# Linear attention and SwiGLU in one kernel: two stretches of small-tile matmuls of group 1 joined into one

## The chip, the cores and the metric

One core of one Trainium2 chip. The metric is device microseconds from the first to the last instruction of the core as the host sees it, median of several executions; a traced execution also has a span, which is 1.7 to 1.9 us shorter. The engines are called PE (TensorE; PEld is its loading of weights), DVE (VectorE), ACT (ScalarE), POOL (GpSimd) and SP (the sync engine, which here issues DMA). PSUM is the memory that PE writes its results to, in banks; SBUF is the memory that holds operands.

## The reference, cut to what matters

```python
def phi(x):
    return np.where(x > 0, x, np.exp(x) - 1.0) + 1.0
q_p, k_p = phi(q), phi(k)                            # 8 batches, 8 heads, 576 x 64
kv  = np.einsum('bhsd,bhse->bhde', k_p, v)           # "k.v": one 64x64 result per head
z   = np.sum(k_p, axis=2)
num = np.einsum('bhsd,bhde->bhse', q_p, kv)          # "q.kv"
den = np.einsum('bhsd,bhd->bhs', q_p, z) + 1e-06     # "q.z"
x   = num / den                                      # 4608 tokens x 512
out = (silu(x @ w_gate) * (x @ w_val)) @ w_out       # "first layer", "second layer"
```

The tokens are worked on in 9 groups of 512. The two layers are matmuls of the full 128x128 array with 512 moving columns, called large here. The attention products k.v, q.z and q.kv use 64x64 tiles of the array, called small. Attention for later tokens is slipped in between the four tiles of a group's second layer.

## The kernel before

A k.v of one batch is 72 small matmuls; both k.v and the products with q are issued by these helpers:

```python
def kv_corner(b, lp, t, first, last):
    ps = kvp[b]
    for j in range(J):                       # J = 9
        for l2 in range(2):
            for hh in range(2):              # four 64x64 corners of the array
                rows = slice(C * hh, C * hh + C)
                nc.tensor.matmul(out=ps[hh][D * l2:D * l2 + D, D * lp:D * lp + D],
                                 lhsT=t[b % 2][rows, lp, j, D * l2:D * l2 + D],
                                 rhs=vr[b % NB][rows, 2 * lp + l2, D * j:D * j + D],
                                 start=(first and j == 0), stop=(last and j == J - 1))

def kv_all(b):                               # k.v of batch b
    kvp[b] = pair()                          # next pair of PSUM banks of a ring of four
    for lp in range(2):
        kv_corner(b, lp, kp, True, True)

def num(g, lp):                              # q.kv
    ps = nump[(g, lp)] = pair()
    ...
```

`r_copy` copies k.v from PSUM to SBUF as R, here with ACT; q.kv uses R as its weights. The block of group 1 (`b1` = 2, `b2` = 3):

```python
def block(g):
    b1, b2 = g + 1, g + 2
    if b1 == 2:
        kv_all(b2)
        for lp in range(2):
            corners(kvp[b2], Zr[1], 1, lp, 7, 9, 2 * P + P * lp)      # q.z
        lnrd(kvp[b2], 0, 2 * P, 4 * P)                                # 1/den on ACT
        for lp in range(2):
            num(b1, lp)                                               # q.kv
            ...
        r_copy(b2, 0, 2, "AA")
...
    for t in range(4):                       # tiles of the second layer
        ...
        if t == 1 and g == 1:
            kv_all(b1)
            r_copy(b1, 0, 2, "AA")
        if t == 3:
            block(g)
        ...
        lay2(g, t)                           # 12 large matmuls
        l2_out(g, t, ...)
```

## Time and profile before

| | kernel before |
|---|---|
| median time | 313.73 us (313.45 to 314.19, 3 runs) |
| span of the traced execution | 311.8 us |
| PE busy, granted clock | 305.4 us (98%), 0.997 |
| DVE, ACT busy | 205.1 us, 152.7 us |
| second layer of group 1, first matmul of tile 0 to first of tile 3 | 70.08 to 80.07 us: 9.99 us |
| the same to the first large matmul of group 2 | 70.08 to 82.78 us: 12.70 us ("the stretch") |

PE is busy throughout and ends the chain, so the question is not which engine is the slowest but what stands in PE's queue and with which gaps. The lines for this are in the prediction.

### The profile page before, as it was taken

The page shows a single profiled execution, that of the slowest core. Times are in us where ns is not written, and L with a number is a line of the kernel's source. Part 1 is how long each engine was busy: PE and PEld are TensorE (multiplying, and loading weights), DVE is VectorE, ACT ScalarE, POOL GpSimd, SP SyncE. Part 2 cuts the span into 40 slices and gives each one's busy share as a digit, 9 for nine tenths or more (in the row PEclk, how much of TensorE's full clock was granted, in tenths as well). Part 3 has the DMA queues.
Part 4 walks back from the last instruction along what each step waited for, and adds up shares of the span by engine and source line. Part 5 has one row for each costly group of instructions (what it writes and reads, how often), then busy time and mean ns, then how long its engine had stood idle before and what let it go on. Part 6 is the DMA issues. An engine that isn't in the chain of part 4 may idle for free.

```text
span 311.8 us, 5565 instructions
## 1 busy us (share of the span) xinstructions
PE 305.4 (98%) x2206; PEld 142.0 (46%) x2206; DVE 205.1 (66%) x361; ACT 152.7 (49%) x231; POOL 48.7 (16%) x73
## 2 busy tenths in 40 slices
PE   7999999999999999999999999999999999999994
PEld 3444454444544454445444544454444444444442
DVE  4855878999599658976697759874981434143410
ACT  4865959538733844374536643574330333033311
POOL 8745444400000410041000500000000000000000
PEclk9999999999999999999999999999999999999998
DMA  8999999999502593239512990323032300240014
GB/s 216 196 198 200 206 206 236 235 206 148 116 15 39 98 196 109 40 58 189 156 38 41 132 233 13 63 52 87 0 75 60 78 1 1 45 92 0 2 34 101
DMA packets 41178, 32.80 MB, mean 105 GB/s; under 512 B 16448, under 2 KB 36160, under 8 KB 41152
## 3 DMA queue, kind: packets, MB, share of 16 engines
q0 software_dynamic: 20480, 18.29, 37.4%
q1 hardware_dynamic: 20592, 14.13, 19.1%
q8 instruction: 17, 0.28, 0.3%
q14 instruction: 9, 0.07, 0.1%
q10 hardware_dynamic: 80, 0.03, 0.0%
HBM read 37.75 MB, written 9.44 MB: 151 GB/s over the span
## 4 chain that ended last, share of the span: by engine, by line
PE 95%; DVE 2%; DMA 1%; SPq 0%; issue 0%; ACT 0%; DVEq 0%
PE pp L292 58%; PE pp L299 30%; PE pp L276 2%; PE pp L254 2%; PE pp L185 2%; DMA q<-in_q_dram 1%; DVE qT L454 1%; PE pp L124 1%; DVE xT L425 0%; PE pp L412 0%; PE pp L212 0%; PE pp L374 0%; DVE osb L322 0%; SPq L333 0%; DVE qp L467 0%
## 5 line engine op out<-in xcount | busy, mean ns | idle before, releaser
L120 ACT ACTIVATE sil<-pp 128x512 f16<-128x512 f32 x108 | 63.4, 597 | 100.8 <-PE pp L292 98.4
L292 PE MATMUL pp<-xT,wg 128*128 128x512 f16 x416 | 106.8, 379 | 0.0
L292 PE MATMUL pp<-xT,wv 128*128 128x512 f16 x416 | 106.8, 379 | 0.0
L285 DVE SCALAR_TENSOR_TENSOR hT<-pp,sil 128x512 f16<-128x512 f32 x108 | 72.3, 681 | 48.0 <-PE pp L292 35.3
L299 PE MATMUL pp<-wo,hT 128*128 128x512 f16 (+2 forms) x444 | 97.1, 373 | 0.6 <-DVE osb L322 0.6
L299 PEld LDWEIGHTS <-hT 128*128 128x128 f16 x444 | 41.9, 98 | 49.9 <-issue 2.1
L292 PEld LDWEIGHTS <-wv 128*128 128x128 f16 x416 | 40.7, 98 | 49.1
L292 PEld LDWEIGHTS <-wg 128*128 128x128 f16 x416 | 40.7, 98 | 48.5
L322 DVE TENSOR_SCALAR osb<-pp 128x512 f32<-128x512 f32 (+1 forms) x19 | 12.9, 681 | 31.1 <-PE pp L299 26.7
L120 ACT ACTIVATE osb<-pp 128x512 f32<-128x512 f32 (+1 forms) x18 | 10.3, 574 | 34.8 <-PE pp L299 34.8
L120 ACT ACT_TABLE_LOAD x13 | 16.7, 1283 | 2.5 <-PE pp L292 2.4
L120 ACT ACTIVATE ek<-kr 128x1152 f16<-128x1152 f16 x16 | 17.8, 1157 | 0.1
L710 POOL COPY gate<-qT 128x1 f16<-128x1 f16 x4 | 1.5, 374 | 95.9 <-DMA qT<-qp 95.9
L229 DVE TENSOR_TENSOR qp<-qp,rden 128x1152 f16<-128x1152 f16 x12 | 16.2, 1347 | 0.0
L220 DVE TENSOR_REDUCE den<-prod 128x18 f32<-128x1152 f16 x12 | 16.1, 1342 | 0.0
L120 ACT ACTIVATE eq<-qr 128x1152 f16<-128x1152 f16 x14 | 15.6, 1151 | 0.1
L271 DVE TENSOR_SCALAR xT<-pp 128x512 f16<-128x512 f32 (+1 forms) x14 | 8.8, 667 | 6.8 <-PE pp L254 6.8
L103 POOL DMA_DIRECT2D vr<-in_v_dram x16 | 11.8, 740 | 8.8 <-DMA wo<-in_moe_w_out_dram 2.4
L103 POOL DMA_DIRECT2D kr<-in_k_dram x16 | 11.5, 722 | 7.9 <-DMA wo<-in_moe_w_out_dram 1.9
L159 DVE TENSOR_TENSOR kp<-ek,kp 128x1152 f16<-128x1152 f16 x15 | 11.4, 758 | 0.5
L147 DVE TENSOR_SCALAR ek<-ek 128x1152 f16<-128x1152 f16 x16 | 8.0, 500 | 5.0 <-ACT ek L120 5.0
L103 POOL DMA_DIRECT2D qr<-in_q_dram x14 | 10.1, 724 | 5.6 <-DMA qr<-in_q_dram 2.6
(86 smaller groups left out, 180.0 us busy)
## 6 DMA issues: line engine op xcount, KB each, us to landing
out_dram<-osb SPq DMA_DIRECT2D x70, 128.0 KB, 2.8
kr<-in_k_dram POOLq DMA_DIRECT2D x16, 288.0 KB, 8.7
vr<-in_v_dram POOLq DMA_DIRECT2D x16, 288.0 KB, 9.7
qr<-in_q_dram POOLq DMA_DIRECT2D x14, 288.0 KB, 11.6
wg<-in_moe_w_gate_dram POOLq DMA_DIRECT2D x5, 256.0 KB, 9.5
wv<-in_moe_w_val_dram POOLq DMA_DIRECT2D x5, 256.0 KB, 10.1
q<-in_q_dram SPq DMA_DIRECT2D x2, 576.0 KB, 4.2
wo<-in_moe_w_out_dram POOLq DMA_DIRECT2D x2, 512.0 KB, 12.4
```

The source lines that it names most:

```text
L103: nc.gpsimd.dma_start(out=dst[b % NB][:, 2 * lp:2 * lp + 2, :], in_=src[b].rearrange("(l a) (c j) d -> (a c) l (j d)", a=2, j=J)[:, 2 * lp ...
L120: nc.scalar.activation(out=out, in_=in_, func=func, bias=bias, scale=scale)
L147: nc.vector.tensor_scalar(out=a, in0=a, scalar1=1.0, scalar2=None, op0=ALU.min)
L159: nc.vector.tensor_tensor(out=a, in0=ek[b % 2][:, lp, :, :], in1=a, op=ALU.add)
L185: nc.tensor.matmul(out=ps[hh][D * l2:D * l2 + D, D * lp:D * lp + D], lhsT=t[b % 2][rows, lp, j, D * l2:D * l2 + D], rhs=vr[b % NB][rows, 2 ...
L220: nc.vector.tensor_reduce(out=den[:, c, :], in_=prod[:, :, :].rearrange("p j (l d) -> p (j l) d", d=D), axis=AX.X, op=ALU.add)
L229: nc.vector.tensor_tensor(out=qv, in0=qv, in1=rden[:, c, :].unsqueeze(2).to_broadcast([P, 2 * J, D]), op=ALU.mult)
L271: nc.vector.tensor_scalar(out=dst, in0=ps[l2][:, c0:], scalar1=1.0 / SC, scalar2=None, op0=ALU.mult)
L285: nc.vector.scalar_tensor_tensor(out=hT[g % 2][:, fb, :], in0=ps[1][:, :], scalar=SC, in1=s[:, :], op0=ALU.mult, op1=ALU.mult)
L292: nc.tensor.matmul(out=ps[h][:, :], lhsT=w[:, c, P * fb:P * fb + P], rhs=xT[g % 2][:, c, :], start=(c == 0), stop=(c == 3))
L299: nc.tensor.matmul(out=l2p[(g, t)][:, n0:n1], lhsT=hT[g % 2][:, fb, P * t:P * t + P], rhs=wo[:, fb, n0:n1], start=(fb == 0), stop=(fb == F ...
L322: nc.vector.tensor_scalar(out=o[:, n0:n1], in0=ps[:, n0:n1], scalar1=1.0 / SC, scalar2=None, op0=ALU.mult)
```

## The change

The intent: batch 2's k.v stood alone between tiles 0 and 1, and PE loses time at each change between large and small tiles. Moved into the block, it shares one entry and one exit with the k.v of batch 3, q.z and q.kv. One of the two q.kv now takes over the banks of batch 2's k.v, so the ring of banks comes out as before but for two pairs that change places.

```diff
-    def num(g, lp):
-        ps = nump[(g, lp)] = pair()
+    def num(g, lp, p=None):
+        ps = nump[(g, lp)] = pair(p)
...
         if b1 == 2:
+            kv_all(b1)
+            r_copy(b1, 0, 2, "AA")
             kv_all(b2)
...
-                num(b1, lp)
+                num(b1, lp, kvp[b1] if lp else None)
...
-                if t == 1 and g == 1:
-                    kv_all(b1)
-                    r_copy(b1, 0, 2, "AA")
```

## The prediction

> **What bounds the kernel now.** I read the busy table and the slices of the page first, then the chain of waits in order of time, then the timeline of group 1's second layer, then the matrix engine's waits. From the page:
>
> ```profile
> PE 305.4 (98%) x2206; PEld 142.0 (46%) x2206; DVE 205.1 (66%) x361; ACT 152.7 (49%) x231; POOL 48.7 (16%) x73
> PE   7999999999999999999999999999999999999994
> PEclk9999999999999999999999999999999999999998
> PE 95%; DVE 2%; DMA 1%; SPq 0%; issue 0%; ACT 0%; DVEq 0%
> ```
>
> TensorE (PE) is busy in every slice after the first, at the full granted clock (0.997), and 95% of the chain that ends last is PE work; no other engine is above 66%. Busy alone would not prove that it is never held up, so I asked who PE waited for from 55 to 310 us. The only answer is 0.6 us for an output copy at the very end. So after the start the kernel is one queue of matmuls, and time can only come from what stands in that queue or from gaps between its entries. A large matmul (128x512) starts every 0.216 us: the chain has 96 of them in 20.72 us.
>
> The part that the change touches, in the chain of waits (start, length, what):
>
> ```profile
> 70.24 2.59 PE pp L299 x12
> 72.83 0.73 PE pp L185 x72
> 73.56 5.29 PE pp L299 x24
> 78.85 0.73 PE pp L185 x72
> 79.58 0.55 PE pp L254 x23
> 80.14 2.69 PE pp L299 x12
> ```
>
> L299 is the second layer, four row tiles of 12 large matmuls. Between tiles 0 and 1 stand the 72 small (64x64) matmuls of batch 2's k.v; between tiles 2 and 3 stand the block: 72 of batch 3's k.v and the 24 of q.z and q.kv. So this group has **two islands of small-tile work**, four changes between full-array and 64x64 work. The later groups already have one island each: at 111.43 the chain shows 16 q.kv then 72 k.v in 0.56 + 0.67 = 1.23 us.
>
> What an island costs beyond its own work must be read by starts, because ends of matmuls are modelled. The PE timeline of this stretch (start, length, what):
>
> ```profile
> 70.08 2.75 PE L299 MATMUL pp<-wo,hT 128*128 128x512 f16 x12
> 72.76 0.80 PE L185 MATMUL pp<-vr,kp 64*64 64x64 f16 x72
> 73.50 5.35 PE L299 MATMUL pp<-wo,hT 128*128 128x512 f16 x24
> 78.78 0.80 PE L185 MATMUL pp<-vr,kp 64*64 64x64 f16 x72
> 79.40 0.30 PE L254 MATMUL pp<-qT,Zr 64*64 64x128 f16 x8
> 79.51 0.62 PE L254 MATMUL pp<-qT,R 64*64 64x384 f16 x16
> 80.07 2.76 PE L299 MATMUL pp<-wo,hT 128*128 128x512 f16 x12
> ```
>
> The reader is to see: 12 large ones from 70.08 would let the next start at 70.08 + 12 x 0.216 = 72.67, but the first small one starts at 72.76, 0.09 us late. The isolated island runs to 73.50, so it takes 73.50 - 72.67 = **0.83 us** of the queue. The same 72 matmuls inside the block, followed by more small ones, go from 78.78 to 79.40: **0.62 us**. The entry into the block shows the same lateness: 73.50 + 24 x 0.216 = 78.68 against 78.78, 0.10 us. In the view of waits, the weight loads sit idle 0.42 us before each island, once put down to "issue" and once to the vector engine's sum for z; the same length both times says that it is the change of tile shape, not a missing operand.
>
> **What the Trainium skill says.** "TensorEngine Tiling (Array Packing)", section Key Properties, says that changing the tiling mode, though not the tile, drains TensorE. The trace agrees in kind: 0.09 to 0.10 us is lost on entry, and (0.83 - 0.62) - 0.09 = 0.12 us on exit; the page gives no length. "TensorE: Matmul & The Clock Gate", Part 2 (what happens when you issue a matmul), says that weight loads are pulled ahead of running matmuls while matmuls stay in program order. The trace agrees: a large weight load starts about 0.21 us before its matmul (72.24 against 72.45), but the first small one starts with its own matmul at 72.76. So the stretch cannot be hidden by running ahead. The spec table at the head of the same page calls ScalarE a strict first-in, first-out queue of depth 8, which matters for where the moved copies of R stand on it.
>
> **The change part by part.**
>
> *Work removed or added: none.* The order of instructions has 4414 PE rows in both programs and the same counts elsewhere. On PE, 72 small matmuls move from behind tile 0 to just ahead of batch 3's k.v. On ScalarE (ACT), the two copies of R for batch 2 move from ahead of tile 1's output copy to behind tile 2's and ahead of the logarithms. The vector, GpSimd and sync orders do not differ.
>
> *Buffers.* There are four pairs of PSUM banks. Call them A, B, C, D in ring order at tile 0. Before: tiles 0 and 1 in A, k.v of batch 2 in B, tiles 2 and 3 in C, k.v of batch 3 in D, q.kv in A and B. After: tiles 2 and 3 take B, k.v of batch 2 takes C, q.kv takes A and, by the new argument, C again. The ring that group 2 inherits is the old one with B and C exchanged, so no later matmul gets a more recently used pair than before.
>
> *PE gain.* The isolated island of 0.83 us becomes 0.62 us inside the block: **-0.21 us**, one entry and one exit less.
>
> *New dependency.* The q.kv of batch 2 needs R of batch 2, which was copied at 76.03, more than 3 us ahead of use at 79.51. Now k.v, copy and use follow each other. My timetable for the new kernel, by starts: 36 large ones from 70.08 end at 77.85; plus 0.10 entry, k.v of batch 2 runs 77.95 to 78.57, batch 3's 78.57 to 79.19, q.z 79.19 to 79.30 (79.40 to 79.51 before). R must be there by 79.30. ACT takes tile 2's output from about 0.21 us after 77.85, so 78.06 to 78.66 (0.60 each). It then needs the end of k.v of batch 2. A 256-column matmul that began at 59.61 released ACT at 59.92, 0.31 us later, and 192 fewer columns at 0.216/512 us each take 0.08 us off, so 0.23 us after the last small one's start at 78.56: about 78.79. The two copies took 0.43 us together, so they end at 79.22. A hand-over to PE took about 0.05 us at the start of the kernel (vector result at 14.80, matmul at 14.85). R is usable at about 79.27, 0.03 us ahead of need, too close to call. I put **+0.05 us** on it, between nothing and some 0.15.
>
> *ACT behind it.* The logarithms started 0.32 us after q.z (79.72 against 79.40), so at 79.51 now; the copies end at 79.22 and do not delay them. ACT's chain to x of group 2 shifts left with the block, and its margin stays.
>
> *Sum:* -0.21 + 0.05 = -0.16 us. The tail from 80.07 on is PE alone, so it should come through whole: 313.73 - 0.16 = **313.57 us**.
>
> **The rivals.**
>
> 1. *The R copy becomes a new wait that eats the gain.* For: the margin above is 0.03 us, and ACT is strictly in order behind a 0.60 us output copy. Against: 0.73 us of PE work (batch 3's k.v and q.z) lies between, and the copy is short. If it goes badly, 0.2 to 0.3 us of wait, and the time is 313.7 to 313.9.
>
> 2. *Another operand is late because the block comes 0.2 us earlier.* Batch 3's k is ready on the vector engine at 77.70, and would be needed at 78.57. The transposes of q for batch 2 are issued at 69.2 and 74.8 and land 3.2 to 6.2 us later; as PE used the second by 79.9 it cannot be the 6.2, so it landed at about 78.0 against 79.3. Group 2's x: the vector engine's last multiply starts at 82.74 for two, ending 83.22, and PE wants its third and fourth chunk at 83.21 and 83.43, a margin of 0.2 us for each. That is thin, but it is tied to the logarithms, which move with the block. If the ACT chain moves less than PE, up to 0.2 us is lost: 313.8.
>
> 3. *The drains do not depend on islands as I think*, and 0.83 against 0.62 is the pitch of that particular k.v. Then nothing is gained: 313.73.
>
> 4. *A much larger effect*, of the clock or of DMA. The clock is full throughout and no transfer feeds PE after the start, so a 2% change (6.3 us) has nothing to come from: the whole stretch moved is 0.83 us, 0.26% of the time.
>
> **Range and chances.** The mechanism gives 313.4 to 313.9. Three runs of the kernel before already spread from 313.45 to 314.19, so run to run scatter is larger than the effect; I widen to 313.0 to 314.2 for that. Even the full island would be 0.3%, so within 2% is near certain.
>
> **What would show it.** In the changed kernel's timeline: no small matmuls between tiles 0 and 1, so 36 large ones start without a gap from 70.08 to 77.85; then 144 k.v ones in about 1.24 us, with one idle stretch of weight loads (0.42 us) ahead of them and none between the two batches; tile 3 at about 79.9 instead of 80.07; the first matmul of group 2 at 82.6 instead of 82.78. Rival 1 shows as a wait of q.kv for ACT's copy of R, or as a gap between q.z and q.kv beyond 0.11 us; rival 2 as a gap inside group 2's first eight matmuls. The prediction is wrong if tile 3 starts no earlier than before, or if the later groups' pitch of 0.216 us changes.

## The result, and the profile after

The changed kernel took 313.69 us (median of 4 runs, 313.49 to 314.06), the kernel before 313.59 (4 runs, 313.40 to 314.19). The ratio is 1.0001, with a 95% interval from 0.9984 to 1.0019: the same. (A ratio here is the mean time of one kernel's fast runs over that of the other's of the same rounds, so it is not quite the ratio of the medians.) So the time agrees with the forecast, 313.57, but the forecast was of a small gain, and the trace must say whether it was there.

From the changed kernel's page, the busy row, the slices and the chain:

```profile
PE 305.7 (98%) x2206; PEld 142.5 (46%) x2206; DVE 204.6 (66%) x361; ACT 152.7 (49%) x231; POOL 48.6 (16%) x73
PE   7899999999999999999999999999999999999994
PE 95%; DVE 2%; DMA 2%; SPq 0%; issue 0%; ACT 0%; DVEq 0%
```

Nothing has changed in kind. The span of this execution is 312.3 us against 311.8, and 0.36 us of that is the start: its tile 0 began at 70.44 instead of 70.08. The chain of waits, same columns as in the prediction, over the part that was changed:

```profile
70.61 7.77 PE pp L299 x36
78.38 1.55 PE pp L185 x144
79.93 0.73 PE pp L254 x20
80.66 2.70 PE pp L299 x12
```

The order is as intended: 36 large matmuls with nothing between them, then 144 of k.v, then q.z and q.kv. By starts, from PE's timeline:

```profile
70.44 7.93 PE L299 MATMUL pp<-wo,hT 128*128 128x512 f16 x36
78.31 1.62 PE L185 MATMUL pp<-vr,kp 64*64 64x64 f16 x144
79.74 0.41 PE L254 MATMUL pp<-qT,Zr 64*64 64x128 f16 x8
80.00 0.66 PE L254 MATMUL pp<-qT,R 64*64 64x384 f16 x16
80.59 2.76 PE L299 MATMUL pp<-wo,hT 128*128 128x512 f16 x12
```

Tile 3 starts 80.59 - 70.44 = 10.15 us after tile 0, where it was 9.99 before: **0.16 us later, not 0.16 us earlier**. The stretch to group 2 is 12.86 us, before 12.70. Each part by starts, beside the prediction's timetable (the 36 large ones, 36 x 0.216 = 7.78 us, are equal in all):

| part, us | before | predicted | changed |
|---|---|---|---|
| first entry (before: of the lone k.v) | 0.09 | 0.10 | 0.09 |
| k.v of batch 2 (before: with its own exit) | 0.73 | 0.62 | 0.68 |
| second entry | 0.10 | none | none |
| k.v of batch 3 | 0.62 | 0.62 | 0.76 |
| q.z | 0.12 | 0.11 + 0.05 for R | 0.26 |
| q.kv with the exit | 0.55 | 0.56 | 0.59 |
| sum | 2.21 | 2.06 | 2.37 |

(The sums are taken before rounding.) The second entry and an exit are indeed gone. But the same small matmuls, which need 0.62 us in an island of their own batch, now need more, and q.z twice its time. What holds them up? The view of waits names no engine for it. The copies of R, which I had feared, were done in time. ACT's timeline, with the idle time before in brackets:

```profile
78.42 0.60 ACT L120 ACTIVATE osb<-pp 128x512 f32<-128x512 f32 x1 [1.43 <-PE pp L299]
79.17 0.45 ACT L120 ACTIVATE R<-pp 128x128 f16<-128x128 f32 x2 [0.16 <-PE pp L185]
```

They end at 79.62, before even q.z begins at 79.74, so q.kv cannot have waited for them at 80.00.

Looking at every single start shows where it goes. Small matmuls come in fours, one for each corner of the array: the four start 3 to 4 ns apart, the next four 32 ns after the first of them. After some 50 matmuls the pattern becomes an even 8 to 9 ns, with weight loads at the same pace. And there are holes. This list, worked out from the traced starts, has every gap of 60 ns or more inside the stretch, by the number of the matmul that it precedes:

```
before, lone k.v (72):    none
before, block (96):       84: 137   92: 138
changed (168):            72: 87   102: 79   150: 86   152: 82   156: 117   164: 94
```

The last two of each block are within q.kv, whose 384 columns keep the array busy (137 ns before); they are not losses. The other four are: 87 ns at the junction of the two k.v, and three of about 80 ns, at places where nothing awaited was late. Each less the 8 ns (at the junction 25) that would stand there anyway, they make 0.29 us; the rest of the loss is in shorter gaps. At the junction stands a separate semaphore instruction (a wait that did not fit on the matmul itself, for batch 3's v). The view of k.v's source line, first of the kernel before and then of the changed one, each limited to the block, gives count, duration, and first and last start:

```profile
L185 PEldq EVENT_SEMAPHORE  x1: 51/51/51, 74.8 to 74.8; - x1
```
```profile
L185 PEldq EVENT_SEMAPHORE  x1: 51/51/51, 78.9 to 78.9; - x1
```

Before, PE's sequencer dealt with it at 74.8, four microseconds ahead of use and under large matmuls. Now it comes up at 78.9, exactly at the junction. That gave the theory to test: **in a long stretch of small matmuls PE uses up instructions as fast as its front end (the fetching and handing out of instructions) supplies them, so the reserve that it builds up under large matmuls runs out, and then every delay of the front end shows.** The rivals: a wait for R after all; the new place or banks of k.v; an array that itself slows in long small-tile work; and chance.

### The profile page after: what moved, and what is told of

It reads as the page before. It is cut to its first block, busy times and chain, and to the rows that moved or that the text cites. A ratio compares the mean times of both kernels' runs of the same rounds, so it can differ in the third digit from the quotient of the medians.

```text
span 312.3 us, 5565 instructions
## 1 busy us (share of the span) xinstructions
PE 305.7 (98%) x2206; PEld 142.5 (46%) x2206; DVE 204.6 (66%) x361; ACT 152.7 (49%) x231; POOL 48.6 (16%) x73
## 4 chain that ended last, share of the span: by engine, by line
PE 95%; DVE 2%; DMA 2%; SPq 0%; issue 0%; ACT 0%; DVEq 0%
PE pp L292 58%; PE pp L299 30%; PE pp L276 2%; PE pp L254 2%; PE pp L185 2%; DMA q<-in_q_dram 2%; DVE qT L454 1%; PE pp L124 1%; DVE xT L425 0%; PE pp L412 0%; PE pp L212 0%; PE pp L374 0%; DVE osb L322 0%; DVE qp L467 0%; DVE kp L143 0%; SPq L333 0%
```

## The experiments

"Stretch" is the measure of the table: 12.70 us before, 12.86 changed. The run-to-run scatter of the whole time is larger than what is sought. Most of the experiments are one traced execution each. How far the stretch scatters can be read from the three kernels of experiments 6 and 9 that leave group 1 as it was before: 12.67 us in each.

**1. The changed kernel again.** No edit.

> The changed kernel once more, to see what repeats. Measure, called the stretch here: from the start of group 1's first second-layer matmul to the start of group 2's first first-layer matmul; 12.70 us in the kernel before, 12.86 in the changed one. Theory (the small-tile stretch of 168 matmuls runs ahead of what PE's sequencer can hand it): the same holes at the same places, 0.09 us between the two k.v, 0.12 us in the middle of the second, 0.17 us around the end of q.z; stretch 12.80 to 12.92; time same within 0.1%. Rival (the holes are chance of that one execution): the holes move or vanish, stretch near the 12.49 that the islands alone would give.

Time 313.60 us (5 runs), ratio 1.0006, interval 0.9993 to 1.0018; stretch 12.88 us. The sum repeats, but the places only in part: holes at 63 (82 ns), 72 (86), 111 (84), 112 (85), and none in q.z. So the junction is fixed, the number of other holes is steady at three, and where they fall moves. Chance placement, then, but not a chance loss. One loss more lies just behind the stretch, where the measure does not see it: the third large matmul of group 2 began 0.50 us after the first instead of 0.43. It uses the third chunk of x, and DVE had begun to multiply that chunk only 0.33 us earlier. The same 0.33 us stands there in experiments 5, 7 and 9 (changed kernel), where this matmul was 0.06 to 0.10 us late; where it was on time, the distance was 0.42 us or more. So this was a wait for x, rival 2 of the prediction, in the changed kernel's second traced execution, though not in its first.

**2. q.kv with an old R**, so that it can't wait for the new copy (the result is wrong: relative error 0.41; `p_old` is set once the block of group 1 is reached).

```diff
-                corners(ps, R[b % 3], b, lp, j0, j1, c0)
+                corners(ps, R[1 if b == 2 and g == 2 and p_old[0] else b % 3], b, lp, j0, j1, c0)
```

> The changed kernel, but q.kv of batch 2 reads the R of batch 1, written long before, so it need not wait for the fresh copy (wrong result on purpose). Theory (feed of PE): R was ready at 79.62 and q.z only began at 79.74, so nothing changes; from the first q.z to the first q.kv stays near 0.26 us, stretch near 12.86. Rival (my prediction's rival 1, wait for the copy of R): q.z to q.kv falls to the 0.12 us of the kernel before, and the stretch to about 12.7.

Stretch 12.84 us; holes at 72 (86), 102 (80), 153 (77), 154 (85), 157 (76), 166 (60). From q.z to q.kv is 0.12 us this time, but the holes went one step on, into q.kv. By that single number the rival looked right; by the stretch and the holes it is out: taking the dependency away gained 0.02 to 0.03 us against the changed kernel.

**3. Four large matmuls between the two k.v**, late place and late R kept.

```diff
-            kv_all(b1)
-            r_copy(b1, 0, 2, "AA")
             kv_all(b2)
...
+                if g == 1 and t == 2:
+                    l2_open(g, t)
+                    for fb in range(FB):
+                        if fb == 8:
+                            kv_all(b1)
+                        l2_mm(g, t, fb)
+                    l2_out(g, t, "A")
+                    r_copy(b1, 0, 2, "AA")
+                    continue
```

> The changed kernel with the last 4 large matmuls of tile 2 moved between k.v of batch 2 and k.v of batch 3: two islands again, all else (banks, late R, order on ScalarE) as in the changed kernel. Theory (a long unbroken small-tile stretch outruns the feed): the second island is like that of the kernel before, k.v of batch 3 0.62 us to q.z, q.z 0.12 us to q.kv, stretch about 12.70. Rival (the late place of k.v or its banks slow the block): the holes stay in the second island and the stretch gets longer than the changed kernel's by one island, to about 13.05.

A miss of my own: stretch 13.07 us. I had put the copies of R behind tile 2's output copy on ACT, and there they ran at 79.34 to 79.78; q.kv then really waited (holes of 190 and 170 ns before its first matmuls). It shows what rival 1 of the prediction costs when it does happen, about 0.4 us. Its k.v of batch 3 had no hole. The mended edit moves the line `r_copy(b1, 0, 2, "AA")` up, to follow `kv_all(b1)` inside the loop:

> The run with 4 large matmuls between the two k.v again, mended: there the copies of R stood behind tile 2's output copy on ScalarE, ran at 79.34 to 79.78 and made q.kv wait; here they stand ahead of it. Theory (PE's front end runs dry in a small-tile stretch longer than about 100 matmuls, and 4 large ones let it fill again): no hole over 60 ns but the two of the kernel before, k.v of batch 3 0.62 us, q.z 0.12 us, stretch 12.70. Rival (late place or banks of k.v): stretch near 12.9 or above.

Stretch 12.70 us, that of the kernel before to the nanosecond (12.696). PE's timeline:

```profile
69.97 7.07 PE L299 MATMUL pp<-wo,hT 128*128 128x512 f16 x32
76.97 0.80 PE L185 MATMUL pp<-vr,kp 64*64 64x64 f16 x72
77.70 1.04 PE L299 MATMUL pp<-wo,hT 128*128 128x512 f16 x4
78.67 0.80 PE L185 MATMUL pp<-vr,kp 64*64 64x64 f16 x72
79.29 0.30 PE L254 MATMUL pp<-qT,Zr 64*64 64x128 f16 x8
79.40 0.62 PE L254 MATMUL pp<-qT,R 64*64 64x384 f16 x16
79.96 2.76 PE L299 MATMUL pp<-wo,hT 128*128 128x512 f16 x12
```

The k.v of batch 2 comes after 32 of the 36 large matmuls, in the same banks. R was copied 1.0 us ahead of q.kv, where the changed kernel left 0.4 us; that the age of R does not matter is what experiment 2 showed. With four large matmuls between, k.v of batch 3 takes 0.62 us again (78.67 to 79.29) and q.z 0.11. So neither place, banks nor R is the cause; the length of the unbroken stretch is, by this execution and by experiment 7.

**4. One island cut into twelve.** In the kernel before, batch 2's k.v is spread over tiles 0 and 1, 4 or 8 small matmuls after every second large one.

```diff
+                    for fb in range(FB):
+                        l2_mm(g, t, fb)
+                        if fb % 2 == 1:
+                            i = 6 * t + fb // 2
+                            for u in range(3 * i // 2, 3 * (i + 1) // 2):
+                                kv_unit(b1, u)
```

> The kernel before with batch 2's 72 k.v matmuls cut into 12 islands, one after every second large matmul of tiles 0 and 1, instead of one. Theory (each entry and exit costs 0.21 us as read): 11 x 0.21 = 2.3 us longer, stretch about 15.0, time 315.9, ratio about 1.007. Rival (the 0.21 us is not the change of shape but something of that one island): stretch near 12.7 and the same time.

Time 316.03 us against 313.50, ratio 1.0082 (1.0066 to 1.0097); stretch 15.16 us. Eleven more islands cost 15.16 - 12.70 = 2.46 us, 0.22 us each; the time agrees, 2.53 us. The price of entry and exit in the prediction (0.21) was right, and is seen by the clock, not only in the trace.

**5. The waits of the junction taken ahead**, by a dummy matmul inside tile 2 that waits for batch 3's v, half of its k and the bank:

```diff
+                        if fb == 8:
+                            nc.tensor.matmul(out=ring[1][0][:, 448:512], lhsT=kp[1][:, 0, 8, :],
+                                             rhs=vr[0][:, 1:3, 0:32], start=True, stop=True)
```

> The changed kernel plus one dummy matmul inside tile 2 that waits for batch 3's v, for its first half of k and for the bank, so that the weight loads at the junction of the two k.v carry no wait (its result is not read). Theory (waits of the junction are handled by PE's sequencer in line, 51 ns for the separate semaphore instruction): the junction falls from 87 ns to about 22 ns, the dummy costs about 0.05 us, the holes of about 80 ns further on stay; stretch about 12.85. Rival (the junction is a real wait for data): it stays at 87 ns or more.

The junction fell from 87 to 25 ns, the dummy cost 29 ns, and two holes of 85 and 89 ns stayed (at 110 and 111); stretch 12.81 us. So the 87 ns were the handling of a wait for something long there, not the wait.

**6. The effect made large enough for the clock.** In groups 2 to 5 of the kernel before, 72 more k.v matmuls (`kv_dup`: the previous batch's, into other columns, not read) either join the block of 88 or stand as an island between tiles 1 and 2.

```diff
                 # in the block
+                kv_dup(b1, ring[0])
                 kv_all(b2)
...
                 # or, in the other kernel, ahead of tile 2
+                if t == 2 and g > 1 and b2 < B:
+                    kv_dup(b1, ring[2])
```

> The effect made large enough for the clock: the kernel before with 72 more k.v matmuls (the previous batch's, result not read) in the blocks of groups 2 to 5, in one stretch with the 88 that stand there. Theory (front end runs dry): one stretch of 160 costs what two islands would or more, about 0.95 us each, 4 x 0.95 = 3.8 us more than before, 317.3. Rival (fewer islands are simply cheaper, as I predicted): 4 x 0.62 = 2.5 us more, 316.0.

> The partner of the run before it: the same 72 extra matmuls in groups 2 to 5, but as an island of their own between tiles 1 and 2. All theories: 0.83 us each, 4 x 0.83 = 3.3 us more than before, 316.8. The difference of the two tells them apart: front end runs dry: the one with islands is the faster by 0.3 to 0.7 us, or they tie; islands alone: it is the slower by 4 x 0.21 = 0.84 us.

In the block: 319.73 us, ratio 1.0207 (1.0185 to 1.0228). As islands: 316.82 us, ratio 1.0102 (1.0088 to 1.0115). Both against a kernel before of 313.56. So the joined form is the *slower* by 2.91 us, where fewer entries alone would make it 0.84 us faster. The islands cost what was worked out, 3.26 us for four. For the joined form even my theory expected too little (317.3). What happens inside its four stretches explains a small part: with entry and exit they sum to 8.82 us, the partner's eight islands to 8.53, so 0.29 us. The rest is two stalls among large matmuls, after the small ones:

```profile
116.07 1.03 PE L303 MATMUL pp<-xT,wg 128*128 128x512 f16 x4
116.94 0.81 PE L303 MATMUL pp<-xT,wv 128*128 128x512 f16 x3
118.32 0.38 PE L303 MATMUL pp<-xT,wv 128*128 128x512 f16 x1 [0.57 <-issue]
...
214.41 0.39 PE L310 MATMUL pp<-wo,hT 128*128 128x512 f16 x1
216.52 1.67 PE L310 MATMUL pp<-wo,hT 128*128 128x512 f16 x7 [1.72 <-issue]
```

"Issue" is idle time for which the profile shows nothing awaited. By starts, 117.37 to 118.32 and 214.41 to 216.52 are 0.95 and 2.11 us where 0.22 is normal: 0.73 + 1.89 = 2.62 us lost. With the 0.29 that makes 2.91, the whole difference of the two traced executions (2.9 us between their spans). The five runs of the joined form went from 319.42 to 321.26 us, its partner's four from 316.76 to 317.01; only one of each is traced here, so whether other runs have the same two stalls is not shown. Shortly before both, a block of instructions was fetched. The DMA view of 213.8 to 215.3 us has this row (packets, MB, share of 16 engines):

```profile
q8 instruction: 1, 0.02, 5.8%
```

In the trace's own records this is a packet of 16,384 bytes that starts at 213.83 and takes 1.40 us; the other stall has one at 116.00, 0.96 us. So both fetches had ended, 1.29 and 1.36 us before the delayed matmul began. The partner has such packets too, one at 214.09 us, and no stall there:

```profile
212.16 0.63 PE L265 MATMUL pp<-qT,R 64*64 64x384 f16 x16
212.62 0.81 PE L185 MATMUL pp<-vr,kp 64*64 64x64 f16 x72
213.36 2.76 PE L310 MATMUL pp<-wo,hT 128*128 128x512 f16 x12
215.96 0.27 PE L223 MATMUL pp<-zs,ob 128*128 128x256 f16 x1
```

"Runtime: NRT & Kernel Launch", section Instruction fetch mechanics, of the Trainium skill says that instructions come in blocks of 16 KiB (256 instructions), fetched while the current ones run, and that this is mostly hidden. The size agrees; 160 small matmuls with their weight loads are 320 instructions in about 2.1 us, and in two of four stretches it was not hidden. No run tests by itself that the fetch is the cause, but the records say more than that the two are near each other. Counted in the trace, the delayed matmuls are the 1,119th and the 2,015th; with their weight loads that is 1,792 instructions apart, 7 blocks of 256. The widened kernel of experiment 9 stalls at the same two matmuls, 1.31 and 1.33 us after such a packet has ended. So the stalls belong to the borders of the fetched blocks. The small holes do not: in the changed kernel no packet of this queue is under way between 75.6 and 80.6 us, and the holes stand at 78.99 to 80.00.

**7. The cut at another place**: both k.v ahead of the last large matmul of tile 2, then q.z and q.kv.

```diff
+                        if fb == 11:
+                            kv_all(b1)
+                            r_copy(b1, 0, 2, "AA")
+                            kv_all(b2)
+                        l2_mm(g, t, fb)
```

> Two islands again, but cut elsewhere: both k.v (144 small matmuls) ahead of the last large matmul of tile 2, then that large one, then q.z and q.kv (24). Theory (the front end runs dry beyond about 60 to 100 small matmuls without a large one): the first island still has the junction of 87 ns and one or two holes of about 80 ns, the second has none but its own two of 0.14 us; stretch 12.86 to 12.95. Rival (only the end of the long stretch, that is q.z and q.kv behind fresh results, makes the holes): 144 matmuls in 1.24 us without holes, stretch 12.70.

The 144 alone have the junction (85 ns) and holes at 66 (137), 120 (81) and 121 (99), so the holes belong to the length and not to q.z or q.kv; behind the one large matmul the 24 have none but their own two (153 ns) and one of 70 ns behind their first four, as the widened k.v of experiment 9 has it too. The stretch, 13.14 us, was longer than I had said, 0.44 more than before. Junction and holes are 0.35 of it (each less the 8 ns, at the junction 25, that would stand there anyway); 0.03 is a wait ahead of group 2 for a copy on ACT; the rest is in shorter gaps.

**8. An attempt at a better version**: the kernel of experiment 5 with q.z between the two k.v.

```diff
-            kv_all(b2)
+            kvp[b2] = pair()
             for lp in range(2):
                 corners(kvp[b2], Zr[1], 1, lp, 7, 9, 2 * P + P * lp)
+            for lp in range(2):
+                kv_corner(b2, lp, kp, True, True)
```

> An attempt at a version better than both: the changed kernel with the waits taken ahead by the dummy matmul, and q.z between the two k.v instead of behind them, so that its 128-column matmuls give the front end a little time. Theory: the junction of 87 ns is gone and perhaps one of two holes; stretch 12.65 to 12.80, so about the kernel before at best. Rival (the holes fall anywhere after about 100 matmuls, whatever the order): as waits_ahead, 12.81.

A miss: stretch 12.92 us, with holes at 103 (150 ns), 150 (137) and 151 (92). The eight matmuls of q.z in between did not take the holes away, and the rival, 12.81, was nearer. No version that I ran beat the kernel before.

**9. More work for the array, the same number of instructions.** First in the joined form of experiment 6 (128 columns instead of 64 in the extra matmuls), then in the changed kernel itself, in batch 2's k.v.

```diff
-                nc.tensor.matmul(out=ps[hh][D * l2:D * l2 + D, 128 + D * lp:128 + D * lp + D],
+                nc.tensor.matmul(out=ps[hh][D * l2:D * l2 + D, 128 + 128 * lp:256 + 128 * lp],
                                  lhsT=kp[b % 2][rows, lp, j, D * l2:D * l2 + D],
-                                 rhs=vr[b % NB][rows, 2 * lp + l2, D * j:D * j + D],
+                                 rhs=vr[b % NB][rows, 2 * lp + l2, D * min(j, 7):D * min(j, 7) + 128],
```

> As the run with 72 extra matmuls in the blocks of groups 2 to 5, the same number of instructions, but each extra matmul moves 128 columns instead of 64, so the array works longer on each (at least 27 ns more for each four, 4 x 18 x 0.027 = 1.9 us more work in all). Theory (instructions are what runs short, not the array): the large stalls of 0.74 and 1.89 us without a semaphore shrink or vanish, and the time falls below 319.7, to about 317.5 to 319. Rival (the array itself stalls in small-tile work): the stalls stay and the work adds, 321 or more.

And in the changed kernel:

```diff
-            kv_all(b1)
+            kv_wide(b1)      # as kv_all, with w = 128 columns for j < 8, 64 for j = 8:
+                # out=kvp[b][hh][D * l2:D * l2 + D, 128 * lp:128 * lp + w]
+                # rhs=vr[b % NB][rows, 2 * lp + l2, D * j:D * j + w]
```

> The changed kernel with batch 2's k.v made heavier for the array but not for the front end: the same 72 matmuls move 128 columns instead of 64 in 16 of the 18 steps (the second half of the columns is not read). Array time of that part rises from 16 x 0.032 to 16 x 0.054 us, 0.35 us more. Theory (the front end is what runs short): while the array works longer it catches up, so the junction of 87 ns and the holes of about 80 ns behind it go, and the added work is nearly free: k.v of batch 3 0.62 us, q.z 0.12 us, stretch about 12.85, as the changed kernel. Rival (the array itself stalls): the holes stay and the work adds, stretch about 13.2.

In the joined form every hole of the small kind is gone: the four stretches have only q.kv's own gaps, and take 2.27, 2.27, 2.25 and 2.25 us, 9.04 in all against 8.82: 0.22 us more time for 1.7 us more array work (72 steps of four at 56 ns instead of 32, as the other widened kernel shows them). But the time is 319.65 us (319.55 to 322.02, 4 runs), as before the widening: two large stalls, 1.10 and 1.26 us, remain, against my expectation that they would shrink with the rest. They are a different thing from the holes.

In the changed kernel the widened k.v took 0.98 us instead of 0.62, 0.36 us more work, and the stretch grew by only 0.12, to 12.98 us. The junction is gone (18 ns), q.z takes 0.12 us again, and of the three holes one of 69 ns is left; k.v of batch 3 still took 0.75. Two thirds of the added work were free, not all as I had expected. It speaks against the array as the cause, which would have added 0.36 us on top of the holes, and for a limit by the number of instructions. It does not show where that limit sits.

## Why the prediction was right or wrong

- **The time was right, and would have been for almost any mechanism here**: 313.57 forecast, 313.69 measured, and "the same" nearly certain. The argument for that (a stretch of 0.83 us cannot move 313 by 2%) held.
- **What bounds the kernel**: right. PE is full in both, and behind the start of group 2 no later group changed.
- **The price of an island, 0.21 us**: right; 0.22 us over eleven of them, by trace and clock.
- **"The same 72 matmuls inside the block ... 0.62 us"**: the step that failed, the cost of the small matmuls in the joined stretch. I took the pace of a k.v from an island of 96 small matmuls and used it for one of 168. In the long one k.v of batch 2 took 0.06 us more, of batch 3 0.14, q.z 0.14 and q.kv 0.04, about 0.38 us that the sum left out. So -0.21 became +0.16 us. "The prediction is wrong if tile 3 starts no earlier than before" was the test that I set, and on that test the gain was not there.
- **Rival 1, the wait for R, +0.05 us in the sum**: measured 0. R was ready 0.12 us before q.z began; old R gained 0.03 us at most. The sign that the prediction named for it, a gap between q.z and q.kv beyond 0.11 us, did come (0.26), but from holes and not from a wait for R.
- **Rival 2, other operands**: not late in the changed kernel's first traced execution; in the second, group 2's x was late by 0.07 us (experiment 1). The step behind it, "The logarithms started 0.32 us after q.z [...] ACT's chain to x of group 2 shifts left with the block, and its margin stays", failed as well: they started 0.56 and 0.53 us after q.z in the two executions (80.30 against 79.74, 80.02 against 79.49). The margin of x, put at 0.2 us, was 0.14 to begin with: in the kernel before the third large matmul began 0.47 us after DVE began on its chunk, and 0.33 us are needed.
- **Rival 3**, that nothing is gained, is what came, but not for its reason: the changes of tile shape do cost what I read. The saving was given back inside the stretch.
- **A view that I had and did not use**: I noted that weight loads are pulled ahead under large matmuls, and took from it only that small ones can't hide the entry. It could also have raised the question whether a long small-tile stretch lives on a reserve that was built under large matmuls, which is the theory tested above.

What is shown is that the loss comes with the length of the unbroken small-tile stretch. That PE's front end runs short is the theory that fits most of it, not a thing shown. One reading does not follow from it: the semaphore of q.z that the logarithms wait for came 0.23 us after the start of its matmul in the kernel before, and 0.45 and 0.44 us after it in the two executions of the changed one. That is why the logarithms are late. So in the long stretch something behind the start of the matmuls runs late too, and no experiment here tells whether that is a result of the holes or their cause. Still open is also what makes single holes of about 80 ns, and whether the recording of executions has a part in them: timed runs have spans recorded as well. In experiment 6 clock and trace agree (2.91 and 2.9 us), but both come from recorded runs. (The prediction's 4414 PE rows stand in no trace: there are 2206 matmuls and as many weight loads in both kernels, so that nothing was added or removed holds.)

## What to carry to other kernels

Joining islands of small-tile matmuls saves their entry and exit, 0.22 us each here, only while the joined stretch stays short: up to 96 small matmuls came through with at most one hole, those of 144 and more lost about as much as the saved change of shape, or more. Count instructions, not only array time, when work is made of many tiny matmuls (widening them was two thirds free here), and let a few large ones stand between two such stretches: four were enough, though that only kept the time of the kernel before. When a gain is smaller than the run-to-run scatter, measure between two events on the bounding engine, look also just behind the second of them, and build a version that repeats the effect before trusting either the clock or the trace.

## What the Trainium skill lacked or had wrong

- "TensorEngine Tiling (Array Packing)", Key Properties: a change of tiling mode drains TensorE, with no length. Here entry and exit together cost 0.22 us (2.46 us for eleven).
- "TensorE: Matmul & The Clock Gate", in the part on the 56 ns gap: start-to-start never below about 25 ns. With four 64x64 tiles the starts are 3 to 4 ns apart within four and 32 ns from four to four, 8 ns on average, as that page's own Part 3 has it for packed tiles (about 4 ns).
- "Runtime: NRT & Kernel Launch", Instruction fetch mechanics: fetching is hidden because instructions are dispatched at about 20 cycles each. Here a weight load and its matmul were handed out every 8 to 9 ns, about 4 ns an instruction, and stalls of 0.73 to 1.89 us that no semaphore explains stood at the borders of the fetched blocks; the delayed matmul began 1.29 to 1.36 us after the end of a 16,384-byte packet.
- No page has how long a small-tile stretch may be: the first gap of 69 ns or more, junction and q.kv's own apart, stood at the 63rd to 138th small matmul of stretches of 144 to 168, and nowhere in the four stretches of 160 with widened matmuls.
- No page has what a separate semaphore instruction costs in PE's stream: 51 ns, nothing when handled ahead under large matmuls, 87 ns instead of 25 from one matmul to the next when met inside small ones.
